# Running sums of a gated recurrence in float32r halves, a bitwise merge of weight words, and a finer written order on one Trainium2 core

## The chip, the cores and the metric

The kernel runs on one core of one Trainium2 chip. The metric is device time of one execution in microseconds (us); lower is better. Inside the core five queues work side by side: TensorE (PE: matmuls, with a separate row PEld for loading the stationary operand), VectorE (DVE), ScalarE (ACT), GpSimd (POOL) and SyncE (SP), which here issues nearly all the DMA transfers. Each queue takes its instructions in the order in which the program wrote them, and the queues wait for each other through semaphores.

## The reference, cut to what matters

The reference has two blocks. The first is a linear recurrence with a complex gate, per batch (4), head (8) and feature pair (48 x 48), over 768 positions. The second is a feed-forward block with an unusual activation.

```python
mag = sqrt(a_re*a_re + a_im*a_im)
scale = minimum(mag, 0.999) / (mag + 1e-06)
a_re_n, a_im_n = a_re*scale, a_im*scale
for t in range(S):                       # S = 768
    S_re, S_im = ar*S_re - ai*S_im + outer(k[t], v[t]), ar*S_im + ai*S_re
    y[t] = q[t] @ S_re
x = y.transpose(0, 2, 1, 3).reshape(3072, 384)
h = x @ w_in                             # 384 x 2048, given in float64
sp = maximum(h, 0) + log1p(exp(-abs(h)))
out = (h * erf(sp)) @ w_out              # 2048 x 384, given in float64
```

The kernel does not step through time. It writes the product of gates over a stretch of positions as exp(sum of log magnitudes) times a rotation by the sum of angles. So it needs, for every unit of positions, a running sum of the log magnitudes (the "decay") and a running sum of the angles. With these the recurrence becomes attention: queries and keys are scaled and rotated, scores are taken, masked by a triangle, and multiplied with the values; a state carries what lies before the chunk.

## The kernel before, in words

The 3072 positions are cut into 12 units u of 256 positions (three units to a batch), each of two chunks c of 128. A unit passes through short named steps. Each step is a Python generator; one `next` of it emits instructions up to the next `yield`. What runs when is set by hand: a long string ORDER lists the steps' names, and a loop at the end of `quotient_path` walks it:

```python
for nm in ORDER.split():
    ...
    next(steps[nm])
```

Nothing reorders the instructions later, so the place of a name in ORDER fixes the place of its instructions in every queue. Several instructions between two yields stay neighbours on their engine.

The steps that matter here, by the first letter of their names:

- `g` loads the gates a_re and a_im of one chunk into the tiles "ar" and "ai" (L771). The pool `lda` has one buffer for each tile, so the load of unit u+1 waits until the last reader of these buffers of unit u is done.
- `m`, `t`, `o`, `l`, `r` (`g_mag`, `g_tan`, `g_off`, `g_log`, `g_turn`) make the log magnitude "s" and the angle "th" on ACT and DVE, with one look that the angles stay in range. `g_log` is three ACT operations in a row, each on the result of the one before, and two DVE operations likewise (L910, L911).
- `p` (`g_decay`) is the running sum of the decays: one matmul with the triangle `triu` (L954, 128 x 384) into a PSUM tile "sum", and two ACT exponentials of it.
- `a` (`g_angle`) is the running sum of the angles: one matmul with the triangle divided by 2 pi, `turns` (L934). The whole turns are then taken off by two DVE operations (L939, L940: add and subtract a large constant, then subtract). The last row of the chunk before is carried in, for the first three units by a second matmul (L936), later by a small DMA of one row and a one-row DVE addition (L931).
- `s` makes cosine and sine on ACT; `K`, `Q` scale and rotate keys and queries on DVE; `M` moves them by 12 DMAs a chunk; `A`, `S`, `Y` are scores, state and result.
- `h` (`ff_in`, L1079) is the first feed-forward product on PE and a copy on ACT; `x` (`softplus`) is four ACT operations of 128 x 2048, each on the result of the one before; `e` (`erf_times_h`) is one ACT operation and then four DVE operations, L1107 to L1110, each of the last three reading what the one before it wrote. There are 96 such groups.
- `O` is the second product (`ff_out_8` for units 0, 1, 2 and 11, `ff_out_7` for the others). In `ff_out_8` a DVE operation brings the result out of PSUM (L1151).
- `n` (`narrow`) makes float32 weights of float64 ones with integer work on the two 32-bit words: two DVE operations, an ACT multiplication of the low word by 2^-29 (L816), and an integer addition on DVE (L818). `i` and `Z` are looks at the data which decide whether the result stands or another path is taken.
- `u` are matmuls whose result nobody reads; they fill PE at the start.

The "sum" tiles of `p` and `a`, the states of `S` and the results of `Y` share two PSUM buffers.

Of the kernel before, what the change touches and what calls it, by code (L numbers as in the profile page):

```python
# [10 lines left out]
FP = mybir.dt.float32  # L11
U8 = mybir.dt.uint8
# [7 lines left out]
P = 128  # L20
# [28 lines left out]
g0.0 u8_0 u2_40 u2_24 u4_38 u2_41 g0.0 u8_1 u2_39 u4_20 u2_25 u4_21 u2_34 g0.1 g0.1 t0.0 t0.0 o0.0 m0.0 m0.0  # L49
l0.0 l0.0 p0.0 t0.1 t0.1 o0.1 v0.1 n0 n0 u4_2 m0.1 m0.1 u2_23 k0.0 p0.0 K0.0 r0.0 a0.0 a0.0 r0.1 a0.1 q0.0 n0 n0  # L50
Q0.0 s0.0 s0.0 Q0.0 K0.0 qT0.0.1 qT0.0.0 kT0.0.1 a0.1 l0.1 l0.1 p0.1 n1 kT0.0.1 n1 k0.1 g1.0 g1.1 p0.0 g1.1 t1.1
t1.1 qT0.0.1 kT0.0.0 kT0.0.0 n1 n1 p0.1 m1.1 q0.1 Q0.1 m1.1 v0.0 S0.0 A0.0.1 t1.0 g1.0 A0.0.1 t1.0 K0.1 m1.0
m1.0 qT0.0.0 A0.0.0 A0.0.0 Y0.0 n3 n3 s0.1 s0.1 K0.1 kT0.1.0 Q0.1 n3 n3 l1.0 l1.0 p0.0 S0.0 n2 n2 Y0.0 qT0.1.0
p0.1 qT0.1.0 kT0.1.0 l1.1 l1.1 n2 o1.1 A0.1.0 A0.1.0 o1.0 n2 n4 n4 q1.1 g2.1 g2.1 n4 p1.0 n5 v1.1 q1.0 k1.0 p0.1
g2.0 p1.0 p1.1 p1.1 p1.1 g2.0 S0.1 S0.1 k1.1 qT0.1.1 n4 r1.0 Q1.0 qT0.1.1 kT0.1.1 a1.0 a1.0 kT0.1.1 A0.1.1
A0.1.1 n5 n5 r1.1 s1.0 s1.0 Q1.0 S0.1 K1.0 p1.1 n6 m2 v1.0 Q1.1 K1.0 Q1.0 K1.1 Y0.1 n7 v2.1 q2.0 p1.0 K1.0 Y0.1
a1.1 a1.1 t2 t2 n5 h0.1.0 n6 h0.1.0 s1.1 n6 o2 m2 n6 n7 s1.1 Q1.1 n7 n7 S1.0 S1.0 K1.1 h0.0.2 h0.0.2 h0.0.0
h0.0.0 r2 l2 l2 g3.0 M1.0 M1.0 M1.0 h0.0.6 g3.1 h0.0.4 M1.0 A1.0.1 A1.0.1 A1.0.0 A1.0.0 Q1.1 a2.0 a2.0 K1.1 Y1.0
n8 n8 h0.0.4 h0.0.6 x0.0 x0.0 a2.1 a2.1 n8 n8 n9 n9 Y1.0 n9 p1.0 t3 g3.1 g3.0 t3 S1.0 p2.0 p2.0 Q2.0 s2 h0.1.4
o3 h0.1.4 s2 S1.1 S1.1 r3 p2.1 Q2.0 n9 k2.0 K2.0 m3 S1.1 p2.1 m3 l3 h0.1.2 a3.0 x0.0 M1.1 M1.1 M1.1 M1.1 A1.1.0  # L60
# [12 lines left out]
l5 A3.1.1 A3.1.0 A3.1.1 K4.0 A3.1.0 e1.1.0 e1.1.0 g6.0 g6.0 O1.0 O1.2 O1.4 O1.1 O1.3 Y3.1 O1.6 O1.5 O1.7 e1.1.2
e1.1.2 O1.8 O1.10 r5 h2.1.2 h2.0.6 e1.1.6 O1.9 O1.11 Y3.0 e1.1.6 e1.1.4 e1.1.4 Q4.0 a5.0 v5.1 g6.1 p4.0 s4 s4
Q4.0 a5.0 x2.0 a5.0 x2.0 Y3.1 x2.0 x2.0 K4.0 S4.0 Q4.1 Q4.0 a5.0 O0.14 O0.15 a5.1 K4.1 Q4.1 K4.0 a5.1 S4.0
h2.1.0 O1.13 K4.1 e2.0.2 e2.0.2 e2.0.6 e2.0.6 p5.0 p5.0 p5.1 p5.1 e2.0.0 h2.1.0 q5.1 q5.0 g6.1 m6 e2.0.0 e2.0.4
e2.0.4 k5.0 M4.0 M4.0 M4.0 h3.0.6 h3.0.6 a5.1 a5.1 S4.1 O1.12 O1.14 O1.15 h3.0.0 M4.0 K4.1 O1.14 O1.14 A4.0.1
A4.0.1 A4.0.0 A4.0.0 m6 O1.15 Q4.1 t6 t6 K5.0 S4.0 o6 S4.1 h3.0.2 Y4.0 S4.1 M4.1 k5.1 M4.1 M4.1 O2.0 v5.0 p5.0
O1.15 M4.1 x2.1 x2.1 x2.1 x2.1 e2.1.6 e2.1.6 O2.2 O2.4 O2.1 O2.3 O2.5 O2.6 e2.1.4 e2.1.4 s5 s5 K5.0 r6 a6.0 Q5.0
e2.1.0 e2.1.0 h3.0.0 e2.1.2 e2.1.2 Q5.0 Q5.0 K5.0 l6 l6 Q5.1 a6.0 h3.0.2 h3.0.4 h3.0.4 a6.1 x3.0 x3.0 x3.0 x3.0  # L80
K5.1 O2.7 A4.1.0 A4.1.0 A4.1.1 A4.1.1 Q5.1 a6.1 g7.0 h3.1.0 O2.9 O2.11 O2.13 O2.15 O2.15 O2.15 g7.1 O2.8 O2.10
O2.12 O2.14 e3.0.2 e3.0.2 Y4.0 e3.0.0 e3.0.0 e3.0.6 e3.0.4 Y4.1 Y4.1 h3.1.0 p6.0 p6.0 b2 h3.1.6 h3.1.6 e3.0.6
O2.14 e3.0.4 b4 h3.1.4 h3.1.4 h3.1.2 h3.1.2 x3.1 x3.1 x3.1 M5.0 M5.0 g7.0 M5.0 M5.0 a6.1 p6.0 p6.0 b0 S5.0 a6.1
b6 K5.1 f3.0 A5.0.1 A5.0.1 A5.0.0 A5.0.0 Q5.1 S5.0 K5.1 h4.1.6 h4.1.6 x3.1 e3.1.2 e3.1.2 e3.1.0 e3.1.0 h4.0.2 t7
e3.1.4 e3.1.4 Y5.0 h4.0.4 O3.0 O3.1 h4.0.2 h4.0.4 e3.1.6 e3.1.6 O3.1 p6.1 g7.1 t7 m7 m7 O2.14 q6.0 p5.0 S5.0
Q6.0 f3.1 k6.0 K6.0 M5.1 M5.1 M5.1 h4.0.0 q6.1 h4.0.6 M5.1 A5.1.0 Y5.0 s6 h4.0.6 h4.0.0 o7 A5.1.0 A5.1.1 A5.1.1
i0 i0 s6 K6.0 Q6.0 h4.1.2 O3.2 O3.2 i1 i1 K6.0 Q6.0 O3.3 O3.4 Y5.1 O3.5 O3.6 O3.7 p6.1 p6.1 p6.1 l7 l7 h4.1.2
k6.1 Q6.1 x4.0 x4.0 x4.0 x4.0 O3.5 O3.5 O3.4 K6.1 O3.7 v6.0 e4.0.0 e4.0.0 M6.0 M6.0 e4.0.2 e4.0.2 M6.0 h4.1.0
M6.0 h4.1.0 e4.0.6 g8.0 e4.0.6 e4.0.4 e4.0.4 g8.1 v6.1 g8.1 q7.1 Y5.1 r7 h4.1.4 O3.12 S6.0 S6.0 O3.8 O3.9 A6.0.1
O3.10 O3.11 h4.1.4 x4.1 x4.1 x4.1 K6.1 A6.0.0 O3.13 x4.1 g8.0 a7.0 a7.0 a7.0 K6.1 O3.13 a7.0 f4.0 a7.1 k7.1 Q6.1  # L90
A6.0.1 A6.0.0 a7.1 Q6.1 O3.11 M6.1 S6.1 S6.1 e4.1.6 e4.1.6 h5.0.6 h5.0.6 e4.1.2 h5.0.2 h5.0.2 e4.1.2 O3.13 v7.0
M6.1 O4.0 Y6.0 e4.1.4 Y6.0 h5.0.0 e4.1.4 h5.0.0 h5.0.4 e4.1.0 e4.1.0 p7.0 p7.0 h5.0.4 p7.1 O4.1 a7.1 a7.1 m8 m8
f4.1 O3.11 M6.1 k7.0 M6.1 h5.1.6 O4.1 q7.0 S6.1 A6.1.0 A6.1.0 A6.1.1 A6.1.1 Q7.0 i2 i2 O4.2 O4.2 i3 K7.0 p7.1 t8
s7 s7 p7.1 K7.0 i3 K7.0 x5.0 x5.0 x5.0 x5.0 O4.3 O4.4 O4.6 O4.5 Q7.0 Q7.1 O4.5 O4.5 O4.4 t8 o8 Q7.0 e5.0.6
e5.0.6 e5.0.0 e5.0.0 h5.1.6 Y6.1 l8 l8 e5.0.2 e5.0.2 h5.1.4 h5.1.4 O4.8 O4.9 S7.0 h5.1.0 O4.10 O4.7 e5.0.4
e5.0.4 h5.1.2 M7.0 p7.0 p7.0 a8.0 M7.0 M7.0 h5.1.0 S7.0 r8 a8.0 O4.7 Q7.1 K7.1 O4.11 K7.1 O4.11 Y6.1 h6.0.0 a8.0
# [555 lines left out]
def quotient_path(  # L652
# [703 lines left out]
```

## Time and profile before

| | us |
|---|---|
| median of 3 runs (688.05 to 690.98) | 688.54 |
| time of the profiled execution | 687.27 |
| its span in the profile | 685.5 |
| PE busy | 655.0 |
| DVE busy | 619.1 |
| ACT busy | 578.0 |
| POOL busy | 1.1 |
| mean granted TensorE clock | 0.992 |

The span is the time between the first and the last recorded instruction; the 1.8 us beside it lie before and after. Busy time is the union of an engine's instructions, so that two that overlap are counted once. For this reason the durations of the single rows add up to more than the busy time: on DVE 658.6 us in rows against 619.1 us busy. The mean of a row is therefore the latency of one instruction, and not always the time for which it keeps the engine.

### The profile page before, as it was taken

The page shows a single profiled execution, that of the slowest core. Times are in us where ns is not written, and L with a number is a line of the kernel's source. Part 1 is how long each engine was busy: PE and PEld are TensorE (multiplying, and loading weights), DVE is VectorE, ACT ScalarE, POOL GpSimd, SP SyncE. Part 2 cuts the span into 40 slices and gives each one's busy share as a digit, 9 for nine tenths or more (in the row PEclk, how much of TensorE's full clock was granted, in tenths as well). Part 3 has the DMA queues.
Part 4 walks back from the last instruction along what each step waited for, and adds up shares of the span by engine and source line. Part 5 has one row for each costly group of instructions (what it writes and reads, how often), then busy time and mean ns, then how long its engine had stood idle before and what let it go on. Part 6 is the DMA issues. An engine that isn't in the chain of part 4 may idle for free.

```text
span 685.5 us, 12236 instructions
## 1 busy us (share of the span) xinstructions
PE 655.0 (96%) x4680; PEld 560.1 (82%) x4680; DVE 619.1 (90%) x1008; ACT 578.0 (84%) x722; POOL 1.1 (0%) x8
## 2 busy tenths in 40 slices
PE   8689999999999999999999999999999999999995
PEld 7458787777677678898898987988998889998984
DVE  4999999999999999999999989999999899868764
ACT  6998979999999959977999999899897795676660
POOL 0000000000000000000000000000000000000000
PEclk9899999999999999999999999999999999999998
DMA  9978888945253244673525534655633547210020
GB/s 215 239 171 173 144 184 173 201 73 94 47 92 57 50 81 75 146 115 73 138 37 115 136 62 84 160 102 86 160 47 53 141 75 160 79 28 24 1 70 29
DMA packets 295403, 71.80 MB, mean 105 GB/s; under 512 B 282004, under 2 KB 285096, under 8 KB 295336
## 3 DMA queue, kind: packets, MB, share of 16 engines
q1 hardware_dynamic: 293256, 70.53, 50.4%
q8 instruction: 39, 0.64, 0.4%
q10 hardware_dynamic: 2080, 0.39, 0.4%
q14 instruction: 28, 0.23, 0.1%
HBM read 48.82 MB, written 4.75 MB: 78 GB/s over the span
## 4 chain that ended last, share of the span: by engine, by line
DVE 32%; ACT 32%; PE 26%; issue 4%; DMA 3%; SPq 2%; DVEq 0%; POOL 0%; ACTq 0%; POOLq 0%
PE hps L1079 10%; ACT L754 7%; ACT yy L755 7%; ACT z L755 7%; DVE yy L1108 4%; DVE e L1109 4%; DVE h L1110 4%; DVE z L1107 4%; PE Z L1179 2%; ACT e L755 2%; ACT CS L755 2%; PE Y L1179 2%; PE X L1179 2%; PE sc L1017 2%; PE unread L1235 2%
## 5 line engine op out<-in xcount | busy, mean ns | idle before, releaser
L1079 PE MATMUL hps<-xT,w_in_sb 128*128 128x256 f32 x1152 | 263.0, 381 | 3.1 <-ACT h L1082 1.9
L1079 PEld LDWEIGHTS hps<-xT,w_in_sb 128*128 128x128 f32 x1152 | 215.3, 190 | 39.6 <-ACT h L1082 5.6
L754 ACT ACT_TABLE_LOAD x100 | 128.3, 1283 | 3.6 <-issue 2.1
L755 ACT ACTIVATE e<-z 128x512 f32<-128x512 f32 x96 | 58.8, 628 | 37.4 <-DVE h L1110 36.9
L1107 DVE TENSOR_TENSOR z<-z,yy 128x512 f32<-128x512 f32 x96 | 65.7, 685 | 13.3 <-ACT e L755 13.2
L1144 PE MATMUL ops<-w_out_sb,h 128*128 128x384 f32 x224 | 75.3, 487 | 0.0
L1082 ACT COPY h<-hps 128x512 f32<-128x512 f32 x96 | 53.7, 578 | 23.4 <-PE hps L1079 19.3
L1108 DVE SCALAR_TENSOR_TENSOR yy<-z,yy 128x512 f32<-128x512 f32 x96 | 66.4, 692 | 3.3
L1110 DVE SCALAR_TENSOR_TENSOR h<-e,h 128x512 f32<-128x512 f32 x96 | 66.5, 692 | 3.3
L1109 DVE TENSOR_TENSOR e<-e,yy 128x512 f32<-128x512 f32 x96 | 66.4, 692 | 3.3
L1144 PEld LDWEIGHTS ops<-w_out_sb,h 128*128 128x128 f32 x224 | 42.1, 190 | 26.5 <-issue 0.4
L1017 PEld LDWEIGHTS sc<-KQ 96*128 96x128 f32 x384 | 47.6, 194 | 10.7 <-ACT KQ L1008 3.6
L1017 PE MATMUL sc<-KQ 96*128 96x128 f32 x384 | 50.2, 281 | 5.9 <-ACT KQ L1008 3.0
L755 ACT ACTIVATE z<-h 128x2048 f32<-128x2048 f32 x24 | 45.9, 1912 | 5.8 <-issue 4.3
L755 ACT ACTIVATE z<-z 128x2048 f32<-128x2048 f32 x24 | 45.9, 1914 | 0.7
L755 ACT ACTIVATE yy<-yy 128x2048 f32<-128x2048 f32 x24 | 45.9, 1913 | 0.6
L755 ACT ACTIVATE yy<-z 128x2048 f32<-128x2048 f32 x24 | 45.9, 1911 | 0.6
L1066 PE MATMUL y<-A,v 128*32 128x128 f32 x768 | 34.9, 282 | 2.8 <-DVE A L1021 2.1
L1021 DVE TENSOR_TENSOR A<-sc,triu 128x512 f32<-128x512 f32 x48 | 31.8, 680 | 1.5 <-PE sc L1017 1.4
L1028 PEld LDWEIGHTS kv<-v,kt 128*96 128x96 f32 x320 | 29.9, 165 | 3.9 <-ACT pr L755 1.2
L1028 PE MATMUL kv<-v,kt 128*96 128x48 f32 x320 | 29.9, 246 | 0.8 <-ACT pr L755 0.6
L1066 PEld LDWEIGHTS y<-A,v 128*32 128x32 f32 x768 | 21.5, 112 | 10.7 <-DVE A L1021 4.1
(107 smaller groups left out, 1021.7 us busy)
## 6 DMA issues: line engine op xcount, KB each, us to landing
KQ<-X SPq DMA_DIRECT2D x264, 64.0 KB
raw<-in_moe_w_in_dram SPq DMA_DIRECT2D x8, 768.0 KB
raw<-in_moe_w_out_dram SPq DMA_DIRECT2D x8, 768.0 KB
again<-in_moe_w_in_dram SPq DMA_DIRECT2D x8, 768.0 KB
ar<-in_a_re_dram SPq DMA_DIRECT2D x24, 192.0 KB
v<-in_v_dram SPq DMA_DIRECT2D x48, 96.0 KB
k<-in_k_dram SPq DMA_DIRECT2D x24, 192.0 KB
q<-in_q_dram SPq DMA_DIRECT2D x24, 192.0 KB
```

The costliest lines, as they stand in the source:

```text
L754: scalar.preload_act_table_set(sets[0])
L755: scalar.activation(func=func, **kw)
L1017: nc.tensor.matmul(out=ps[:, j, :], lhsT=head("k", g * HG + j, u, c), rhs=head("q", g * HG + j, u, c), start=True, stop=True)
L1028: nc.tensor.matmul(out=kv[0:D2, j, :], lhsT=T["kt", u, c][:, j].rearrange("p u d -> p (u d)"), rhs=side(T["v", u][:, c, j // 2], j % 2), s ...
L1066: nc.tensor.matmul(out=ps[b * QUAD:(b + 1) * QUAD, i, :], lhsT=lhsT, rhs=rhs, start=start, stop=stop)
L1079: nc.tensor.matmul(out=ps[:, e, :], lhsT=w_in_sb[:, (sl * SLAB + i) // 2, kd, e * P:(e + 1) * P], rhs=T["xT", u][:, kd, :], start=(kd == 0 ...
L1082: scalar.copy(out=T["h", u, sl][:, i:i + 2, :], in_=ps)
L1107: vector.tensor_tensor(out=z, in0=z, in1=y, op=OP.mult)
L1108: vector.scalar_tensor_tensor(out=y, in0=z, scalar=-2.0, in1=y, op0=OP.add, op1=OP.mult)
L1109: vector.tensor_tensor(out=e, in0=e, in1=y, op=OP.mult)
L1110: vector.scalar_tensor_tensor(out=h, in0=e, scalar=1.0 / RT2, in1=h, op0=OP.add, op1=OP.mult)
L1144: nc.tensor.matmul(out=ps, lhsT=lhsT, rhs=w_out_sb[:, i, :], start=i == HALF, stop=i == KF - 1)
```

## The change

Five edits are made together.

1. For units 2 to 11 the running sums take their input as two parts in the type float32r, a high part and the rest, and add them with two float32r matmuls (`running`). The decays' parts are made by two DVE operations in `g_log`, the angles' by one ACT and one DVE operation in `g_angle`. Units 0 and 1 keep float32 matmuls; their angle is divided by 2 pi on ACT first. Unit 2 carries its row by DMA like the later ones.
2. The whole turns of an angle are taken off by one ACT operation (adding the large constant as a bias) and one DVE operation.
3. The low word of a weight is shifted and joined by bits in one DVE operation; the ACT multiplication is gone.
4. The result of `ff_out_8` leaves PSUM on ACT. The state's two halves are done by one DVE operation where there were two.
5. Yields are put between operations that stood together, and ORDER is written anew: 2291 names where there were 1756.

The parts use buffers that exist: "hi" that of "y", "lo" that of "ar", and the angle's parts that of "ai". The row carried by DMA goes to "s" where it went to "y".

```diff
+    triu_r = const.tile([P, P], FPR, name="triu_r")
+    vector.tensor_scalar(out=triu_r, in0=triu, scalar1=1.0, scalar2=None, op0=OP.mult)
...
+    def running(ps, hi, lo):
+        nc.tensor.matmul(out=ps, lhsT=triu_r, rhs=hi, start=True, stop=False)
+        nc.tensor.matmul(out=ps, lhsT=triu_r, rhs=lo, start=False, stop=True)
...
     def narrow(i):
-        scalar.mul(out=lo, in_=lo, mul=2.0**-29)
-        yield
-        vector.tensor_tensor(out=dst.bitcast(U32), in0=a, in1=lo, op=OP.add)
+        vector.scalar_tensor_tensor(out=dst.bitcast(U32), in0=lo, scalar=29, in1=a, op0=OP.logical_shift_right, op1=OP.bitwise_or)
         yield
...
     def g_log(u, cc=ALL):
         vector.tensor_tensor(out=s, in0=s, in1=y, op=OP.subtract)
         yield
+        if u < 2:
+            return
+        hi, lo = (whole(pool, nm, u, [P, C, DM], tag=tag, dtype=FPR)[:, cc[0]:cc[1]] for pool, nm, tag in ((tmp, "hi", "y"), (lda, "lo", "ar")))
+        vector.tensor_scalar(out=hi, in0=s, scalar1=1.0, scalar2=None, op0=OP.mult)
+        yield
+        vector.tensor_tensor(out=lo, in0=s, in1=hi.bitcast(FP), op=OP.subtract)
+        yield
...
     def g_angle(u, c):
-        nc.tensor.matmul(out=ps, lhsT=turns, rhs=th, start=True, stop=not (goes_on and on_pe))
-        if goes_on and on_pe:
-            nc.tensor.matmul(out=ps, lhsT=ident[:, P - 1:P].to_broadcast([P, P]), rhs=prev, start=False, stop=True)
+        if u > 1:
+            parts = lda.tile([P, 2, DM], FPR, tag="ai", name="parts")
+            hi, lo = parts[:, 0], parts[:, 1]
+            scalar.mul(out=hi, in_=th, mul=1.0 / TAU)
+            yield
+            vector.scalar_tensor_tensor(out=lo, in0=th, scalar=1.0 / TAU, in1=hi.bitcast(FP), op0=OP.mult, op1=OP.subtract)
+            yield
+            ps = ps_b.tile([P, DM], FP, tag="b", name="sum")
+            running(ps, hi, lo)
...
-        vector.tensor_scalar(out=F, in0=ps, scalar1=MAGIC, scalar2=MAGIC, op0=OP.add, op1=OP.subtract)
-        vector.tensor_tensor(out=F, in0=ps, in1=F, op=OP.subtract)
+        act(out=F, in_=ps, func=AF.Identity, bias=magic)
+        yield
+        vector.scalar_tensor_tensor(out=F, in0=F, scalar=MAGIC, in1=ps, op0=OP.subtract, op1=OP.subtract)
         yield
...
     def g_decay(u, c):
-        nc.tensor.matmul(out=ps, lhsT=triu, rhs=T["s", u][:, c, :], start=True, stop=True)
+        if u < 2:
+            nc.tensor.matmul(out=ps, lhsT=triu, rhs=T["s", u][:, c, :], start=True, stop=True)
+        else:
+            running(ps, T["hi", u][:, c, :], T["lo", u][:, c, :])
...
     def erf_times_h(u, sl, i):
         vector.tensor_tensor(out=z, in0=z, in1=y, op=OP.mult)
+        yield
         vector.scalar_tensor_tensor(out=y, in0=z, scalar=-2.0, in1=y, op0=OP.add, op1=OP.mult)
+        yield
         vector.tensor_tensor(out=e, in0=e, in1=y, op=OP.mult)
+        yield
         vector.scalar_tensor_tensor(out=h, in0=e, scalar=1.0 / RT2, in1=h, op0=OP.add, op1=OP.mult)
...
     def ff_out_8(u):
-                vector.tensor_scalar(out=o[:, jj * DM:(jj + 1) * DM], in0=ps, scalar1=-RT2, scalar2=None, op0=OP.mult)
+                scalar.mul(out=o[:, jj * DM:(jj + 1) * DM], in_=ps, mul=-RT2)
```

A stretch of ORDER around the first slab of unit 2 shows the effect of the yields. Before:

```
e2.0.2 e2.0.2 e2.0.6 e2.0.6 p5.0 p5.0 p5.1 p5.1 e2.0.0 h2.1.0 q5.1 q5.0 g6.1 m6 e2.0.0 e2.0.4
```

After:

```
e2.0.0 e2.0.0 e2.0.0 h2.1.6 e2.0.2 e2.0.2 e2.0.0
e2.0.2 e2.0.0 e2.0.2 e2.0.2 O1.12 p5.0 p5.0 p5.0 h3.0.6 h3.0.6 O1.14 e2.0.6 e2.0.6 p5.1 O1.3 O1.5 a5.0 a5.0 a5.0
```

## The prediction

> **What bounds the kernel now.** I read the page's busy shares first, then a table by stage, then the order of time on PE and DVE.
>
> ```profile
> PE 655.0 (96%) x4680; PEld 560.1 (82%) x4680; DVE 619.1 (90%) x1008; ACT 578.0 (84%) x722; POOL 1.1 (0%) x8
> ```
>
> PE is full to 96%, but DVE with 90% is close. The table by stage (span, then busy time of PE, PEld, DVE, ACT, POOL, granted clock, DMA share) shows where each limits:
>
> ```profile
> 0.00:86.00 86.00, 70.90 (x538) 57.59 (x539) 73.18 (x128) 74.72 (x125) 1.09 (x8) 0.96 0.88 189
> 86.00:206.00 120.00, 118.08 (x793) 89.16 (x792) 114.21 (x175) 112.64 (x144) 0.00 (x0) 1.00 0.63 123
> 206.00:343.00 137.00, 133.62 (x989) 112.32 (x988) 131.93 (x215) 118.05 (x139) 0.00 (x0) 1.00 0.47 92
> 343.00:480.00 137.00, 134.84 (x966) 121.61 (x965) 131.05 (x210) 130.87 (x159) 0.00 (x0) 1.00 0.50 98
> 480.00:583.00 103.00, 102.65 (x782) 93.97 (x782) 97.10 (x157) 83.82 (x97) 0.00 (x0) 1.00 0.51 107
> 583.00:651.00 68.00, 68.00 (x486) 63.28 (x485) 53.44 (x86) 46.24 (x51) 0.00 (x0) 1.00 0.13 32
> 651.00:685.50 34.50, 26.87 (x136) 22.21 (x134) 18.20 (x43) 11.67 (x12) 0.00 (x0) 0.94 0.15 49
> ```
>
> PE lacks 15.1 us in the first 86 us (a chain of short waits), 7.8 us from 86 to 651, and 7.6 us at the end. From 86 to 480 DVE stands at 96% beside PE: both bind. From 480 on PE binds alone. So less work on PE pays only if DVE gets no more work in the middle.
>
> Two stretches in order of time (start, duration, instruction) give what an instruction really keeps its engine for. On PE:
>
> ```profile
> 519.67 8.04 PE L1079 MATMUL hps<-xT,w_in_sb 128*128 128x256 f32 x36
> 527.54 0.81 PE L954 MATMUL sum<-s,triu 128*128 128x384 f32 x2
> 528.19 2.75 PE L1079 MATMUL hps<-xT,w_in_sb 128*128 128x256 f32 x12
> 538.42 1.48 PE L1028 MATMUL kv<-v,kt 128*96 128x48 f32 x16
> 539.84 0.43 PE L1066 MATMUL y<-A,v 128*32 128x128 f32 x8
> ```
>
> One float32 running sum of 384 columns is two instructions and holds PE for 528.19 - 527.54 = 0.65 us. On DVE, two groups of `e`:
>
> ```profile
> 521.46 0.69 DVE L1110 SCALAR_TENSOR_TENSOR h<-e,h 128x512 f32<-128x512 f32 x1
> 522.07 0.68 DVE L1107 TENSOR_TENSOR z<-z,yy 128x512 f32<-128x512 f32 x1
> 522.79 0.69 DVE L1108 SCALAR_TENSOR_TENSOR yy<-z,yy 128x512 f32<-128x512 f32 x1
> 523.51 0.69 DVE L1109 TENSOR_TENSOR e<-e,yy 128x512 f32<-128x512 f32 x1
> 524.24 0.69 DVE L1110 SCALAR_TENSOR_TENSOR h<-e,h 128x512 f32<-128x512 f32 x1
> ```
>
> L1107 starts 0.61 us after L1110, whose result it does not read. L1108, L1109 and L1110 each read what stands right before them and start 0.72 to 0.73 us after it. A neighbour that depends costs 0.11 to 0.12 us more than one that doesn't.
>
> **The change part by part.**
>
> *PE.* Units 2 to 11 have 20 decay and 20 angle sums: 40 x 0.65 = 26.0 us. Two carry matmuls of unit 2 go: 1.3 us. New: 80 float32r matmuls. The trace has no float32r, so the price has bounds. The row is 0.65 / (384 columns) = 1.69 ns a column. The Trainium skill (FP8 and Floating Point Precision, TensorE Precision Notes) says that true float32 takes four passes through the array, and that "reduced precision" reads 4 bytes and truncates them, which I take as one pass. One pass is then 0.65 / 4 = 0.163 us (an estimate), 80 of them 13.0 us, and PE saves 26.0 + 1.3 - 13.0 = 14.3 us. If a weight load limited it: the L1028 instructions with 48 columns follow each other in (539.84 - 538.42) / 16 = 0.09 us with 96-column loads, so 128 columns need about 0.12 us, still under 0.163; at the full latency of a load (0.190 us) the saving would be 12.1. Two passes each would save 1.3 us; four passes would cost 24.7. I take 14.3. Two more unread matmuls (0.27 us each) lie in the start, where PE waits anyway; were it full there they would cost 0.5.
>
> *DVE, by durations.* Turns of the angle: 24 x (0.545 + 0.558) go, 24 x 0.546 come (row of L1187 from PSUM, 128 x 384): -13.4. Results of `ff_out_8`: 8 x 0.545 = -4.3. State: 72 operations of 192 elements (21.9) become 36 of 384 at about 0.55: -2.1. Weights: 16 x 0.950 become 16 x 0.963: +0.2. New: "hi" of the decays 10 x 0.542 (row L910; up to 0.959 if the new type is slower), "lo" 10 x 0.959 (L911), "lo" of the angles 20 x 0.548, two one-row additions 1.1: +27.1. Sum +7.5 us, at most +11.7.
>
> *DVE, by neighbours.* In the queue before, 390 of 1008 operations read what the one right before wrote (288 of them in `e`, 24 in the turns, 14 in `g_log`, 16 in `narrow`). In the new order I count 155 (113 in `e`). 235 x 0.12 = 28.2 us less. A check of the rule on before: rows add up to 658.6; 618 free neighbours overlap by 0.08 (0.69 - 0.61), 390 lose 0.03: 658.6 - 49.4 + 11.7 = 620.9, against 619.1 busy. DVE needs 7.5 - 28.2 = 20.7 us less, or 598.
>
> Here a rule speaks against the change. The skill (Perfetto Trace Analysis, Optimizing Scalar/DVE Operations) says of every instruction that the second half of its profiled latency overlaps with the next one, and that grouping into larger operations helps a full engine. By that all neighbours are alike, the new order is worth nothing, and the added operations are plain cost: DVE +7.5 in a middle where it already binds, so PE's 14.3 is mostly kept back there and only the PE-bound end from 480 on gains, about 14.3 x 205 / 685 = 4 us. The rows above show that the overlap is lost between dependent neighbours, so I take the trace's 28.2.
>
> *ACT.* Turns: 24 x 0.585 (the `pr` row from PSUM, 0.487, plus 0.10 for a bias held in a tile, as 0.617 against 0.515 in the two CS rows of 384) = +14.0. Angles: 20 x 0.52 and 4 x 0.52 = +12.5. `ff_out_8`: 8 x 0.487 = +3.9. Low words: 16 x 0.918 = -14.7. One table load of 100 goes: -1.3. Sum +14.4, less 57 fewer dependent neighbours (112 to 55) x 0.12 = 6.8: about +8 us. ACT is tight only to 206 us (112.6 of 120); there the low words, all in units 0 to 2, take off as much as ten or twelve chunks add. After that ACT has 10% free. Cost on the path: 0. If that cover fails, at most the 8 us.
>
> *The start.* The chain gates - angle - keys - scores gets, for each of four chunks, one ACT operation (0.52) and one exchange of a DVE operation (0.545) for an ACT one (0.585) with one more change of engine; the turned-about pairs in `g_tan` and `g_log` give back 0.1 each. I take 0, between -3 and +3.
>
> *Waits.* The angle's sum now waits ACT, DVE, PE, ACT, DVE in turn, where it was PE, DVE, DVE. PE's queue behind the sum holds `h`, `O` and `kv` matmuls, which wait with it. Before, PE's waits for "th" and for the row add up to about 3 us. The end is the same chain of `x11.1`, `e11.1`, `O11`; its DVE part is 16 operations, of which some free up (up to 1 us), and the last result leaves by ACT in 0.49 instead of DVE in 0.55. SP issues two more row DMAs (0.6 us each, off the path). The middle's 7.8 us of PE waits may shrink with a freer DVE or grow with the longer chains: I take 0, from -5 to +8.
>
> Sum on the profiled execution: 687.3 - 14.3 = 673.0 us. That execution lay 1.3 us under the median of the runs, so a median may read 673 to 674. I say 673. Measurement can tell about 0.5% (3.4 us) from no change.
>
> **The rivals.**
>
> *The new order also takes out waits.* PE's work is then 655.0 - 14.3 = 641, with a start of 86 us that loses 8 instead of 15 and a middle that loses 4: 641 + 8 + 4 + 7.6 + 1.8 = 662. For it: DVE is relieved by more than PE. Against: the start is a chain of single operations, not of loads.
>
> *float32r does not pay.* Two passes a matmul or a hidden conversion: PE saves 1.3, DVE's relief finds PE full, 687.3 - 1.3 = 686, with a few waits less 684.
>
> *Gate loads come too late (slower).* "lo" lies in the buffer of "ar" and the angle's parts in that of "ai", one buffer each. Before, these were free once `m` and `t` had read them, and the loads of unit 6 stood ahead of the angles of unit 5. In the new order every load from unit 3 on stands behind the last running sum of the unit before, and the PE work between that sum and the first ACT operation on the new gates is only 2 to 9 us for nine units. A load of the same size (192 KB):
>
> ```profile
> 261.11 2.89 DMA k<-in_k_dram
> ```
>
> With three issues of 0.62 us ahead, "ar" lands 4.8 us after its buffer is free. ACT takes its queue in order, so copies of `h` and the softplus wait behind a late gate, and PE waits for the copies. If 3 us of each of nine units come through to PE: 27 - 14.3 = +13, 700 us. It decides from 14.3 / 9 = 1.6 us a unit. Against it: ACT has some 10% free after 206 us, and `O` work on PE needs no ACT.
>
> **How the numbers follow.** Main case, 667 to 680 us: 0.62, likeliest 673. Waits taken out, 655 to 667: 0.18. float32r without gain, 680 to 688: 0.09. Late gates, 688 to 705: 0.11. Eight in ten: 660 to 686, leaving out some 0.06 below and 0.13 above. Faster than 685.1 by the first two and half of the third: 0.84. Slower than 692: 0.09. Between: 0.07.
>
> **What would show it.** Right: two float32r sums start 0.16 us apart, one instruction each; PE busy about 641; DVE busy near 600 although its rows add up to more than 658; L1107 to L1110 mixed from two groups at 0.61 us; PE at 97% or more from 86 us on. Wrong: float32r pairs with two instructions; neighbours that are free but still 0.72 us apart; ACT idle before `s<-ar` for "DMA ar"; PE's waits for ACT's copies of `h` above 20 us in all.

## The result and the profile after

The changed kernel takes 672.29 us (median of 4 runs, 670.72 to 674.11), the kernel before 688.29 us beside it on the same chip (687.94 to 690.98). The ratio is 0.976, with a 95% interval of 0.972 to 0.980: faster by 16 us. The total is the predicted one (673.0). What it is made of is not, as the experiments show.

Busy time, first line of the page of after:

```profile
PE 642.9 (96%) x4680; PEld 558.7 (83%) x4680; DVE 605.5 (90%) x984; ACT 581.5 (87%) x761; POOL 1.1 (0%) x8
```

The table by stage of after (span, then busy time of PE, PEld, DVE, ACT, POOL, granted clock, DMA share and GB/s), cut at the same places up to 583 us:

```profile
0.00:86.00 86.00, 71.28 (x604) 59.26 (x605) 73.63 (x125) 75.36 (x132) 1.09 (x8) 0.98 0.84 196
86.00:206.00 120.00, 117.83 (x808) 92.33 (x810) 117.62 (x183) 117.73 (x154) 0.00 (x0) 1.00 0.59 118
206.00:343.00 137.00, 135.75 (x908) 115.22 (x901) 130.53 (x211) 131.21 (x165) 0.00 (x0) 1.00 0.48 94
343.00:480.00 137.00, 136.54 (x1059) 126.52 (x1058) 130.56 (x208) 124.31 (x159) 0.00 (x0) 1.00 0.52 109
480.00:583.00 103.00, 102.47 (x790) 94.72 (x788) 96.41 (x155) 85.60 (x103) 0.00 (x0) 1.00 0.46 97
583.00:635.00 52.00, 51.62 (x390) 47.94 (x390) 40.18 (x66) 35.31 (x42) 0.00 (x0) 1.00 0.17 39
635.00:669.40 34.40, 27.46 (x139) 22.75 (x137) 16.59 (x40) 12.01 (x13) 0.00 (x0) 0.97 0.08 26
```

PE's work fell by 12.1 us (655.0 to 642.9), its idle time by 4.0 (30.5 to 26.5): 14.7 us of it lie in the first 86 us, 4.8 from there to 635, 6.9 at the end. From 86 to 206 us DVE and ACT are both at 98%, as PE is.

The float32r sums, in PE's order of time in after (start, duration, instruction):

```profile
534.28 2.75 PE L1150 MATMUL hps<-xT,w_in_sb 128*128 128x256 f32 x12
536.68 0.53 PE L911 MATMUL sum<-parts,triu_r 128*128 128x384 f32 x1
537.05 0.34 PE L912 MATMUL sum<-parts,triu_r 128*128 128x384 f32 x1
537.23 0.97 PE L1254 MATMUL Y<-w_out_sb,h 128*128 128x192 f32 x5
```

From 534.28 to 537.23 are 2.95 us. Twelve L1150 take 2.62 of them (36 of their kind took 7.87 us before), so the pair takes 0.33 us, where one float32 sum took 0.65. Each is one instruction.

DVE's order of time in after, where two groups of `e` are mixed:

```profile
303.60 0.68 DVE L1182 TENSOR_TENSOR e<-e,yy 128x512 f32<-128x512 f32 x1
304.32 0.69 DVE L1184 SCALAR_TENSOR_TENSOR h<-e,h 128x512 f32<-128x512 f32 x1
304.93 0.69 DVE L1178 TENSOR_TENSOR z<-z,yy 128x512 f32<-128x512 f32 x1
305.65 0.69 DVE L1180 SCALAR_TENSOR_TENSOR yy<-z,yy 128x512 f32<-128x512 f32 x1
306.26 0.68 DVE L1178 TENSOR_TENSOR z<-z,yy 128x512 f32<-128x512 f32 x1
```

L1184 reads what L1182 wrote and starts 0.72 us after it; L1178 belongs to the other group and starts 0.61 us after its neighbour.

The new operations, among the groups by line of after (operation, shapes, count, busy us, mean ns, idle before):

```profile
L985 DVE SCALAR_TENSOR_TENSOR parts<-th,parts 128x384 fp32r<-128x384 f32 x20 | 11.0, 548 | 1.8 <-ACT parts L983 1.6
...
L958 DVE TENSOR_TENSOR lo<-s,hi 128x768 fp32r<-128x768 f32 x10 | 9.4, 942 | 0.0
...
L956 DVE TENSOR_SCALAR hi<-s 128x768 fp32r<-128x768 f32 x10 | 5.6, 556 | 0.1
```

They cost what float32 operations of the same size cost. And the longest waits of after (engine, what waits, for what: us in total, times, longest):

```profile
DVE z L1178 <- ACT e L786: 22.6, 21, 5.0
ACT e L786 <- DVE h L1184: 22.2, 13, 4.3
ACT h L1153 <- PE hps L1150: 14.8, 9, 2.5
ACT parts L983 <- DVE th L977: 8.3, 6, 5.0
...
ACT th L786 <- DMA ar<-in_a_re_dram: 0.9, 1, 0.9
```

One gate load was late, once, by 0.9 us. In the groups of `e`, ACT and DVE wait for each other for 45 us, beside 50 before (36.9 and 13.2).

A view that the prediction left out is the chain of work that ended last: followed back from the last instruction, at each step to what released it. By engine and by line, of before:

```profile
DVE 32%; ACT 32%; PE 26%; issue 4%; DMA 3%; SPq 2%; DVEq 0%; POOL 0%; ACTq 0%; POOLq 0%
PE hps L1079 10%; ACT L754 7%; ACT yy L755 7%; ACT z L755 7%; DVE yy L1108 4%; DVE e L1109 4%; DVE h L1110 4%; DVE z L1107 4%; PE Z L1179 2%; ACT e L755 2%; ACT CS L755 2%; PE Y L1179 2%; PE X L1179 2%; PE sc L1017 2%; PE unread L1235 2%
```

Of after:

```profile
PE 39%; ACT 34%; DVE 16%; issue 4%; SPq 3%; DMA 3%; DVEq 0%; ACTq 0%
```

Before, PE was busy for 96% of the span and yet only 26% of the chain led over it. Some 32% of it is the exchange between ACT (softplus, `z` and `yy`, then the activation of `e`) and DVE (the four operations that give the buffers back). The experiments show how far such shares can be trusted.

### The profile page after: what moved, and what is told of

Same layout as the page of the kernel before. It is cut to its first block, busy times and chain, and to the rows that moved or that the text cites. A ratio compares the mean times of both kernels' runs of the same rounds, so it can differ in the third digit from the quotient of the medians.

```text
span 669.4 us, 12235 instructions
## 1 busy us (share of the span) xinstructions
PE 642.9 (96%) x4680; PEld 558.7 (83%) x4680; DVE 605.5 (90%) x984; ACT 581.5 (87%) x761; POOL 1.1 (0%) x8
## 4 chain that ended last, share of the span: by engine, by line
PE 39%; ACT 34%; DVE 16%; issue 4%; SPq 3%; DMA 3%; DVEq 0%; ACTq 0%
PE hps L1150 16%; ACT L785 7%; PE ops L1219 6%; ACT yy L786 6%; ACT z L786 5%; ACT CS L786 3%; PE sc L1082 3%; ACT e L786 3%; PE Z L1254 2%; PE X L1254 2%; SPq L1062 2%; PE y L1137 2%; DVE yy L1180 2%; ACT th L786 2%; DVE z L1178 2%
## 5 line engine op out<-in xcount | busy, mean ns | idle before, releaser
L1150 PE MATMUL hps<-xT,w_in_sb 128*128 128x256 f32 x1152 | 261.4, 381 | 1.5 <-ACT h L1153 1.3
L1150 PEld LDWEIGHTS hps<-xT,w_in_sb 128*128 128x128 f32 x1152 | 216.0, 190 | 34.5 <-ACT h L1153 4.3
L1178 DVE TENSOR_TENSOR z<-z,yy 128x512 f32<-128x512 f32 x96 | 64.7, 687 | 23.0 <-ACT e L786 22.6
L1219 PE MATMUL ops<-w_out_sb,h 128*128 128x384 f32 x224 | 77.3, 488 | 0.4 <-ACT out L1226 0.4
L1180 DVE SCALAR_TENSOR_TENSOR yy<-z,yy 128x512 f32<-128x512 f32 x96 | 64.7, 688 | 1.7
L1184 DVE SCALAR_TENSOR_TENSOR h<-e,h 128x512 f32<-128x512 f32 x96 | 64.7, 685 | 1.2
L1182 DVE TENSOR_TENSOR e<-e,yy 128x512 f32<-128x512 f32 x96 | 64.6, 685 | 1.0
```

The lines of the kernel that those rows point to most:

```text
L1150: nc.tensor.matmul(out=ps[:, e, :], lhsT=w_in_sb[:, (sl * SLAB + i) // 2, kd, e * P:(e + 1) * P], rhs=T["xT", u][:, kd, :], start=(kd == 0 ...
L1178: vector.tensor_tensor(out=z, in0=z, in1=y, op=OP.mult)
L1180: vector.scalar_tensor_tensor(out=y, in0=z, scalar=-2.0, in1=y, op0=OP.add, op1=OP.mult)
L1182: vector.tensor_tensor(out=e, in0=e, in1=y, op=OP.mult)
L1184: vector.scalar_tensor_tensor(out=h, in0=e, scalar=1.0 / RT2, in1=h, op0=OP.add, op1=OP.mult)
L1219: nc.tensor.matmul(out=ps, lhsT=lhsT, rhs=w_out_sb[:, i, :], start=i == HALF, stop=i == KF - 1)
```

## The experiments

Time is the median, the ratio is to the kernel before on the same chip, with its 95% interval. Busy and idle time are of each run's profiled execution; PE idle is the span less PE busy. That execution can lie some us from the median (702.43 in new_order, 672.23 in a_turns, 722.11 in a_grouped). Names with "b" start from the kernel before, names with "a" from the changed one; two experiments that are set against each other may come from different chips.

| run | us | ratio | PE busy | PE idle | DVE busy |
|---|---|---|---|---|---|
| before | 688.29 | 1 | 655.0 | 30.5 | 619.1 |
| b_pe | 688.52 | 1.001 [0.999, 1.002] | 647.9 | 37.9 | 618.9 |
| b_chain | 683.44 | 0.993 [0.991, 0.995] | 653.4 | 26.0 | 611.1 |
| b_pe_chain | 682.84 | 0.992 [0.990, 0.995] | 650.8 | 31.3 | 611.3 |
| b_words | 687.83 | 1.000 [0.998, 1.001] | 656.2 | 29.2 | 618.7 |
| new_order | 698.95 | 1.015 [1.011, 1.018] | 663.2 | 37.4 | 601.8 |
| new_order_words | 677.66 | 0.985 [0.982, 0.988] | 653.0 | 21.8 | 601.5 |
| a_mul | 703.14 | 1.020 [1.016, 1.025] | 659.0 | 42.9 | 606.2 |
| a_f32 | 675.75 | 0.981 [0.977, 0.984] | 653.1 | 21.2 | 606.2 |
| a_turns | 675.41 | 0.983 [0.981, 0.985] | 643.1 | 27.4 | 615.9 |
| a_dve | 675.99 | 0.982 [0.979, 0.986] | 645.2 | 28.7 | 615.5 |
| a_chain | 670.44 | 0.977 [0.972, 0.983] | 641.7 | 25.1 | 602.9 |
| a_grouped | 713.89 | 1.036 [1.033, 1.040] | 665.1 | 55.3 | 622.3 |
| after | 672.29 | 0.976 [0.972, 0.980] | 642.9 | 26.5 | 605.5 |

### Parts of the change in the order of before

**b_pe**: float32r sums alone. Each sum is two float32r matmuls, here of the same data.

```diff
-        nc.tensor.matmul(out=ps, lhsT=triu, rhs=T["s", u][:, c, :], start=True, stop=True)
+            for i in range(2):
+                nc.tensor.matmul(out=ps, lhsT=triu_r, rhs=T["s", u][:, c, :].bitcast(FPR), start=True, stop=True)
```

> The kernel before with its own order; only the running sums of units 2 to 11 are two float32r matmuls in place of one float32 matmul (they add the input's rounded high part alone: the second matmul overwrites the first, and the division of the angles by 2 pi is left out). DVE and ACT do the same operations as before. PE has 40 x 0.33 = 13.0 us less. Theory A (PE and DVE both bind in the middle): only part is kept, because from 86 to 480 us DVE stays 95% full; 5 to 9 us faster, 679 to 683 us. Rival B (PE alone binds): the whole 13 us, 675 us. Rival C (float32r saves PE nothing): 688.

Measured 688.52 us: nothing. The table by stage of b_pe for the stretch in which DVE is at 96%:

```profile
206.00:343.00 137.00, 131.70 (x990) 112.43 (x989) 132.07 (x215) 118.20 (x139) 0.00 (x0) 1.00 0.47 92
343.00:480.00 137.00, 132.37 (x963) 120.83 (x963) 131.12 (x211) 130.85 (x159) 0.00 (x0) 1.00 0.50 98
```

PE has 1.9 and 2.5 us less to do there than before, and each stretch holds nearly the same work as before: what PE gave up became waiting. Over the whole span PE loses 7.1 us of work and gains 7.4 us of idle time. Theories A and B, which gave a part or all of it to the time, fall. Theory C has the number, but its reason is false, since the pair is shorter than the float32 sum:

```profile
520.15 8.04 PE L1092 MATMUL hps<-xT,w_in_sb 128*128 128x256 f32 x36 [0.32 <-ACT xT L1081]
527.83 0.70 PE L965 MATMUL sum<-s,triu_r 128*128 128x384 f32 x2
528.39 1.78 PE L1092 MATMUL hps<-xT,w_in_sb 128*128 128x256 f32 x7
```

From 520.15 to 528.39 are 8.24 us; the 36 L1092 take 7.87 of them, so the pair takes 0.37 us. The granted clock hides one to two us at most: b_pe's executions at 0.984 to 0.987 took 686.4 to 688.7 us, those of the kernel before at 0.984 to 0.986 took 688.4 to 690.5, and at 0.990 both lie at 687.4 to 688.8.

**b_chain**: in `e`, the operands are exchanged so that L1108 to L1110 no longer read what stands right before them; places and number of operations stay.

```diff
-        vector.scalar_tensor_tensor(out=y, in0=z, scalar=-2.0, in1=y, op0=OP.add, op1=OP.mult)
-        vector.tensor_tensor(out=e, in0=e, in1=y, op=OP.mult)
-        vector.scalar_tensor_tensor(out=h, in0=e, scalar=1.0 / RT2, in1=h, op0=OP.add, op1=OP.mult)
+        vector.scalar_tensor_tensor(out=y, in0=y, scalar=-2.0, in1=y, op0=OP.add, op1=OP.mult)
+        vector.tensor_tensor(out=e, in0=e, in1=h, op=OP.mult)
+        vector.scalar_tensor_tensor(out=h, in0=h, scalar=1.0 / RT2, in1=h, op0=OP.add, op1=OP.mult)
```

> The kernel before with its own order; in the four DVE operations of each group e the operands are exchanged so that none reads what its neighbour wrote (same shapes, same number; the activation's value is left out). 288 dependent neighbours go, 288 x 0.12 = 34 us of DVE. Theory A: DVE busy falls to about 590, and since PE is full, the time falls only by what PE waited for DVE: 3 to 7 us, 681 to 685. Rival B (PE alone binds): under 2 us, 687. Rival D (the overlap does not depend on who wrote the operand): DVE busy stays 619 and the operations stay 0.72 us apart; 688.

Measured 683.44 us, as expected, but from a smaller relief: DVE busy 611.1, 8.0 us less and not 29. DVE's order of time in b_chain says why:

```profile
516.80 0.69 DVE L1107 TENSOR_TENSOR z<-z,yy 128x512 f32<-128x512 f32 x1
517.51 0.69 DVE L1108 SCALAR_TENSOR_TENSOR yy<-yy 128x512 f32<-128x512 f32 x1
518.12 0.68 DVE L1109 TENSOR_TENSOR e<-e,h 128x512 f32<-128x512 f32 x1
518.84 0.69 DVE L1110 SCALAR_TENSOR_TENSOR h<-h 128x512 f32<-128x512 f32 x1
519.45 0.68 DVE L1107 TENSOR_TENSOR z<-z,yy 128x512 f32<-128x512 f32 x1
```

Only L1109 became free (0.61 us after L1108). L1108 writes `yy`, which L1107 reads, and L1110 writes `h`, which L1109 reads: both still start 0.71 to 0.72 us after their neighbour. These rows alone would also fit a cost that goes with the kind of operation, since a TENSOR_TENSOR stands before each late start. The trace of after speaks against it: there an L1180 of one group follows an L1182 of another six times, the same two kinds in the same order, and starts after 0.60 to 0.61 us each time. One freed neighbour in each of 96 groups, at 0.11, is 10.6 us. So 8.0 us less on DVE brought 4.9 us, while 7.1 us less on PE brought none.

**b_pe_chain**: both together.

> Both of the two edits before together (with what they leave out), order of before. Theory A: each uncovers the other, so the sum is more than the parts: 13 us of PE and about 4 us of waits, 670 to 673 us. Rival B: 675, the same as with float32r sums alone. Rival E (the new order itself, not the lighter load, makes the gain): above 680.

Measured 682.84 us: b_chain's time again. Theory E has the number. float32r pays nothing in this order even with DVE 8 us lighter. What a larger relief would do this run doesn't say: DVE is still busy for 96% of the time from 206 to 480 us (131.68 and 131.12 of 137 us each).

**b_words**: in the order of before, the ACT multiplication goes and the low word is joined by bits.

```diff
-        scalar.mul(out=lo, in_=lo, mul=2.0**-29)
         yield
-        vector.tensor_tensor(out=dst.bitcast(U32), in0=a, in1=lo, op=OP.add)
+        vector.scalar_tensor_tensor(out=dst.bitcast(U32), in0=lo, scalar=29, in1=a, op0=OP.logical_shift_right, op1=OP.bitwise_or)
```

> The kernel before with its own order; only the low words of the weights are shifted and joined in one DVE operation, so 16 ACT operations of 0.92 us (14.7 us) go, all in the first 170 us. Theory A: ACT is full only there and off the path: 0 to 3 us faster, 685 to 688. Rival G (ACT sets the pace of the first 206 us): 6 us or more faster, under 682.

Measured 687.83 us: nothing, although ACT has 12 us less to do. Alone, neither this edit nor the float32r sums are worth anything.

### The new order

**new_order**: ORDER and the yields of after, with the operations of before; places of new operations stay empty. The ACT multiplication is issued just ahead of the DVE addition, which has one place.

> The operations of the kernel before in the new order, with the new yields: float32 running sums (without parts), the whole turns on DVE, low words on ACT, results of the plain units out by DVE, the state's halves apart. Where a step of the changed kernel has no counterpart, the place is empty. Theory H (the order itself makes most of the gain, above all in the first 210 us; the changed kernel with float32 sums, 675.75, then owes its gain to it): 674 to 679 us, the first softplus at 58 to 60 us. Rival A (the lighter operations make it): 683 or more.

Measured 698.95 us: slower than before, and far from the 674 to 679 of theory H, that the order carries the gain by itself. Rival A's 683 or more holds as a number; the next run shows that one operation makes most of it. DVE is relieved as in after (601.8 us). The loss lies at the start. Three engines in order of time in new_order:

```profile
68.76 1.91 ACT L786 ACTIVATE z<-h 128x2048 f32<-128x2048 f32 x1
...
70.80 1.91 ACT L786 ACTIVATE z<-z 128x2048 f32<-128x2048 f32 x1
...
74.02 0.63 ACT L786 ACTIVATE e<-z 128x512 f32<-128x512 f32 x1
74.55 0.86 ACT L848 ACTIVATE raw<-raw 128x768 uint32<-128x768 uint32 x1
75.45 0.96 DVE L849 CUSTOM_DVE_ANT_0 w_in_sb<-raw,word 128x1536 uint16<-128x1536 uint16 x1 [9.27 <-ACT raw L848]
76.32 1.28 DVE L1076 TENSOR_TENSOR A<-sc,triu 128x512 f32<-128x512 f32 x2
...
77.06 0.65 PE L1129 MATMUL y<-A,v 128*32 128x128 f32 x8 [7.26 <-DVE A L1076]
```

The multiplication (L848) stands in ACT's queue behind the first softplus. DVE waits 9.27 us for it with the masks `A` (L1076) queued behind, and PE waits 7.26 us for the masks. One operation in a bad place stops two engines.

**new_order_words**: the same, with the low words joined by bits.

> The operations of before in the order of after, as in new_order, with one thing more from the change: the low word of a weight is shifted and joined by bits in one DVE operation, so the ACT multiplication is gone (new_order issued it right in front of the DVE addition). new_order started its second slab (the second start of a softplus) at 135.9 us, the changed kernel at 111.8, and lost 24 us there; from there to the last slab both need about the same (529 and 523 us). Theory J: those 24 us are the DVE's wait for the ACT multiplication, which stands in ACT's queue behind other work (11.6 and 11.5 us of wait in the trace). Then the first slab starts at 58 to 61 us, the second at 111 to 116, and the time is 672 to 680 us, beside 675.75 of a_f32. Rival K: another old operation makes the start long (the two DVE operations of the turns, the matmul with the divided triangle, the carry by matmul). Then the second slab starts after 125 us and the time is 688 to 700 us.

Measured 677.66 us, as theory J expects; the second slab (what the second softplus works on) starts at 111.83 us (135.90 in new_order, 111.80 in after). The order and this one operation, with all other operations as before, make 10.6 of the 16.0 us (by the ratios 0.985 beside 0.976). In its table by stage PE has no idle time from 206 to 480 us:

```profile
0.00:86.00 86.00, 73.16 (x599) 60.61 (x600) 73.86 (x133) 69.50 (x118) 1.09 (x8) 0.96 0.85 196
...
206.00:343.00 137.00, 137.00 (x944) 115.35 (x943) 131.43 (x219) 127.29 (x154) 0.00 (x0) 1.00 0.49 97
343.00:480.00 137.00, 137.00 (x1047) 124.98 (x1046) 123.64 (x203) 117.66 (x144) 0.00 (x0) 1.00 0.52 108
```

**a_mul**: the counterpart: after, with the ACT multiplication and the DVE addition back at the one place.

> The changed kernel with the low words alone as before: the ACT multiplication by 2^-29 and then the integer addition on DVE, both issued at the place of the one DVE operation (16 of each). Theory J (the order is written for the operation without the step over ACT, and the wait stands in the start, where nothing covers it): the second slab starts 15 to 25 us later than 111.8 and the time is 686 to 698 us. Rival L (the start has slack, new_order lost its time by its other old operations): 670 to 677 us.

Measured 703.14 us, 31 us over after and 5 over theory J's upper end; the second slab starts at 141.25 us, 29 later. new_order and a_mul do not price the multiplication as such: in the order of before it started 0.96 us or more ahead of its reader, in all but one case 1.6 us or more, and taking it away gained nothing (b_words). They show that the new order fits the new operation only.

### float32r, turns and DVE in the new order

**a_f32**: after, with each pair of float32r matmuls replaced by one float32 matmul on the high part. The parts are made as in after.

```diff
-        nc.tensor.matmul(out=ps, lhsT=triu_r, rhs=hi, start=True, stop=False)
-        nc.tensor.matmul(out=ps, lhsT=triu_r, rhs=lo, start=False, stop=True)
+        nc.tensor.matmul(out=ps, lhsT=triu, rhs=hi.bitcast(FP), start=True, stop=True)
```

> The changed kernel with its order, its parts and all its DVE and ACT work, but each running sum of units 2 to 11 is one float32 matmul over the high part (the low part is left out of the sum). PE has 40 x 0.33 = 13.0 us more. Theory A (PE binds): 672.3 + 13 = 685, 682 to 687. Rival E (the new order makes the gain): 672 to 676.

Measured 675.75 us: PE has 10.2 us more to do than in after, and 5.3 us less idle time. In the order of after the float32r pair is worth some 3.5 us, a quarter of what the prediction gave it; theory E has the number. The intervals of the ratios (0.977 to 0.984 here, 0.972 to 0.980 for after) overlap, so the size is rough.

**a_turns**: after, with the large constant added by DVE.

```diff
-        act(out=F, in_=ps, func=AF.Identity, bias=magic)
+        vector.tensor_scalar(out=F, in0=ps, scalar1=MAGIC, scalar2=None, op0=OP.add)
```

> The changed kernel with one thing moved: the large constant that takes the whole turns off an angle is added by DVE and not by ACT, at the same place in the order (24 operations of 128 x 384, 0.58 us each on ACT, about 0.55 us on DVE). new_order_words, which has neither the float32r sums nor edits 2 and 4, stood at 677.7, the changed kernel at 672.3. Theory M (the path runs over ACT in the middle as much as over PE, 34% and 39% of the chain of waits, and DVE has slack): ACT loses 14 us of work, two changes of engine a chunk go, and the time is 667 to 672 us. Rival N (DVE's additions cost as in a_dve, where 10 us more of DVE busy time gave 3.7 us; 13 us give about 5): 675 to 679 us. Within 672 to 675 the step was worth nothing either way.

Measured 675.41 us (672.23 to 677.44): rival N. Moving this step to ACT is worth some 3 us (5 by the ratios). ACT busy falls by 10.0 us (to 571.5), DVE busy rises by 10.4, and the loss is about that of the next run, which adds as much to DVE: the relief of ACT brings nothing to be seen.

**a_dve**: after, with 192 small operations more on DVE, two in each group of `e`.

```diff
+        for t in (off, zeros):
+            vector.tensor_scalar(out=t, in0=t, scalar1=1.0, scalar2=None, op0=OP.mult)
```

> The changed kernel with two more small DVE operations (18 and 24 columns, in place, values unchanged) behind the first operation of each group e: 192 operations, at about 0.1 us some 19 us more of DVE. Theory H' (the new order lives from the free DVE time that it makes): 8 us or more slower, 680 and over. Rival I (DVE has slack in the new order, what was gained is placing and not DVE time): 672 to 676.

Measured 675.99 us, within rival I: 10.0 us more on DVE cost 3.7 us, with intervals that overlap a little. DVE is not the bound of after, but it isn't covered either.

**a_chain**: after, with the operands of b_chain.

> The changed kernel with the operands of group e exchanged as above (the activation's value is left out): the last 113 dependent neighbours in e go, 113 x 0.12 = 13.6 us of DVE. Theory A: DVE has slack after the change, PE binds: within 2 us of the changed kernel, 670 to 673. Rival F (DVE still binds after the change): 5 us or more faster, 667 or less.

Measured 670.44 us, no difference from after that its interval (0.972 to 0.983) can show. But DVE had only 2.6 us less to do, where 13.6 were expected, so theory A was hardly put to the test. DVE's order of time in a_chain:

```profile
304.02 0.68 DVE L1178 TENSOR_TENSOR z<-z,yy 128x512 f32<-128x512 f32 x1
304.74 0.69 DVE L1180 SCALAR_TENSOR_TENSOR yy<-yy 128x512 f32<-128x512 f32 x1
305.35 0.69 DVE L1178 TENSOR_TENSOR z<-z,yy 128x512 f32<-128x512 f32 x1
```

As in b_chain, L1180 overwrites what L1178 reads and starts 0.72 us after it, and L1184 likewise after L1182. Only L1182 behind L1180 became free: 29 such neighbours stand in the trace, 26 of them over 0.7 us apart in after and none in a_chain, which is 2.9 us at 0.11.

**a_grouped**: after, with the four DVE operations of each `e` together at the place of the second.

```diff
-        vector.tensor_tensor(out=z, in0=z, in1=y, op=OP.mult)
         yield
+        vector.tensor_tensor(out=z, in0=z, in1=y, op=OP.mult)
         vector.scalar_tensor_tensor(out=y, in0=z, scalar=-2.0, in1=y, op0=OP.add, op1=OP.mult)
-        yield
         vector.tensor_tensor(out=e, in0=e, in1=y, op=OP.mult)
-        yield
         vector.scalar_tensor_tensor(out=h, in0=e, scalar=1.0 / RT2, in1=h, op0=OP.add, op1=OP.mult)
```

> The changed kernel with its order, but each group e issues its four DVE operations together, at the place of the second. About 175 more dependent neighbours, 175 x 0.12 = 21 us more on DVE, and the first operation comes a little later, the last a little earlier than in the changed kernel. Theory A (the relief of DVE is what lets the lighter PE pay): DVE fills the middle again and takes back 5 to 11 us: 677 to 683. Rival B (PE alone binds): 671 to 674.

Measured 713.89 us, and both theories missed it by over 30. In the profiled execution, 8 us slower than the median, DVE's work rose by 16.8 us and PE's idle time by 28.8. The neighbours explain the first number at most. The rest may come from operations at places that the order didn't mean for them, which is not shown. The run doesn't price the neighbours.

## Why the prediction was right, and where it wasn't

The 673 us were right, but the reason given for them holds in part only: float32r was worth less than forecast and the order more, and that the two errors cancel is luck. Most of the named signs of being right were met too (PE 642.9 us busy, each float32r sum one instruction, groups of `e` mixed at 0.61 us, PE at 98% from 86 us on). They say that the work changed as forecast, not that its saving made the gain.

- **The bound.** "From 86 to 480 DVE stands at 96% beside PE: both bind" is right for what it warns of, and b_pe agrees: less work on PE alone pays nothing. Of "from 480 on PE binds alone" b_pe says little: only four sums of the kernel before stand after the softplus at 488.25 us, worth 1.1 us (0.65 less 0.37 us a pair in b_pe, each), and from there to the end b_pe needs 197.0 us (from 488.76), the kernel before 197.3. The Trainium skill (Perfetto Trace Analysis, Identifying the Most-Contended Engine) says that the matmul's busy share is no good measure of how close PE is to its limit, that the share of weight loads (and the rate of arithmetic) should be read for PE, and that the engine with the highest occupancy comes first. By that the order before is DVE 90%, ACT 84%, PE 82% by its loads. The runs agree for DVE against PE (b_chain: 8.0 us less, 4.9 gained; b_pe: 7.1 us less, nothing). For ACT they don't (b_words: 12.1 us less, nothing), though that work lies in the first 150 us. The chain of waits, with 32, 32 and 26%, does no better for ACT. It doesn't price an edit either: in b_chain PE has 44% of it, and the float32r sums are still worth nothing there (b_pe_chain); in a_f32 it has 77%, and 10.2 us less PE work are worth 3.5.
- **PE's sum.** 14.3 us of work were forecast, 12.1 came (the pair at 0.33 us, as the estimate from four passes against one gave: 2 x 0.163). The size is nearly right. The step that failed is the one after it, putting all of it on the path: it is worth 0 in the old order (b_pe, b_pe_chain) and some 3.5 us in the new one (a_f32).
- **DVE.** Rows: +7.5 forecast; the new rows are as costed. Neighbours: -28.2 forecast. Busy time fell by 13.6, so that with 7.5 of new rows the new order gave back 21.1; with the operations of before it gave 17.3 (new_order). The sign and the 0.61 against 0.72 us are right, the sum was too large, by a third against 21.1 and by more against 17.3. Why the rest stays away isn't settled; the count took a neighbour that only overwrites as free, which b_chain shows it is not, but how many of these the new order has is not known. The check of the rule on the kernel before was kinder than it should have been: 658.6 us are the busy times of the groups of rows added up, while all rows one by one make 663.2, and the check then gives 625.5 for 619.1. The rule that all neighbours overlap alike would have had DVE busier than before; after and new_order show the opposite.
- **Waits, taken as 0.** This term was mis-sized, and on the way over new_order_words it carries most of the gain. In PE's own accounts, span = busy + idle: from before to new_order_words work falls by 2.0 and idle time by 8.7 us; from there to after, work falls by 10.1, while idle time rises by 4.7. From end to end that is 12.1 less work and 4.0 less waiting, which looks like the forecast of 14.3 and 0. Only the run in between shows that the order, with the bitwise merge, saves waiting, and that nearly half of the lighter work turned into waiting.
- **ACT, path 0.** ACT's work rose by 3.5, not 8. The step over ACT for the turns doesn't cost but pays about 3 us (a_turns). That the low words' work offsets the chunks' missed the point: the multiplication's work doesn't matter, its place in ACT's queue does (21 us between new_order and new_order_words, 31 between a_mul and after).
- **The start, 0**, and **the end, 0**: PE's idle time there went from 15.1 to 14.7 and from 7.6 to 6.9. Right for after. But the start is also where a misplaced operation costs most.
- **The rivals.** "The new order also takes out waits" had the right mechanism, with a gain that float32r's was to be added to; the two are not additive. "float32r does not pay" had the right outcome for the old order, by a wrong cause (two passes or a conversion). "Gate loads come too late" fell: 0.9 us in all. Buffers of their own for the parts were not tried.

What stays open: why the old order doesn't profit from less PE work even with DVE 8 us lighter (b_pe_chain), and which of the 2291 places bring the 10.6 us. They may do it through DVE's relief (new_order_words: 17.6 us less work, 10.6 us gained; b_chain: 8.0 and 4.9, both 0.6 us for one). But in the new order 10.0 us more on DVE cost only 3.7 (a_dve), and no run keeps the new places without the relief or the whole relief without the new places.

## What to carry to other kernels

Read the chain of waits beside the busy shares: PE at 96%, with a quarter of the chain, did not repay less work. Take it as a warning and not as a price, since with 44% of the chain it did not either. In queues that run in a written order, an operation and its place are one thing: price an edit in the order that it will have, since the same edit, the bitwise merge of the low words, was worth 0 in one order and 21 to 31 us in the other. And where each engine's time is nearly full, look for what its neighbours in the queue cost before looking for work to take away.

## What the runs showed of the hardware

A neighbour on DVE that overwrites what the one before it reads costs as much as one that reads its result: 0.71 to 0.72 us from start to start against 0.61 (b_chain, 128 x 512; a_chain has it too).

Long waits on PE went together with a lower granted clock, and so cost more than their length. The first stage of new_order:

```profile
0.00:86.00 86.00, 67.42 (x468) 56.16 (x469) 60.30 (x110) 63.65 (x108) 1.08 (x8) 0.82 0.69 166
```

The clock is 0.82 there, 0.96 in new_order_words and 0.80 in a_mul. For the same 4680 matmuls PE is busy for 663.2 us in new_order and 653.0 in new_order_words: some 10 of the 21 us between them. The clock accounts for that size: 0.96 less 0.82 of 67.42 us are 9.4 us (an estimate). The Trainium skill (TensorE: Matmul & The Clock Gate, Part 1) tells of a gate that halves the clock after an idle window; the rows agree in kind, as means over stages, and don't show its steps.

Operations on 18 to 24 columns have rows of 0.168 to 0.170 us and keep DVE for less (a_dve):

```profile
307.73 0.69 DVE L1178 TENSOR_TENSOR z<-z,yy 128x512 f32<-128x512 f32 x1
308.34 0.25 DVE L1180 TENSOR_SCALAR seen<-seen 128x24 f32<-128x24 f32 x2
308.50 0.68 DVE L1182 SCALAR_TENSOR_TENSOR yy<-z,yy 128x512 f32<-128x512 f32 x1
```

Two of them take 0.16 us from start to start, 0.08 each. The 192 added only 10.0 us to DVE's busy time, 0.05 each, since many stand between two dependent neighbours: L1182 (the second operation of a group in this run) starts 0.77 us after the L1178 whose result it reads, where the pair alone takes 0.72.
